# Thresholds and row-sum scaling on GpSimd from the second batch on, and all query, key and value loads on SyncE's queue

## The chip, the cores and the metric

The kernel runs on one core of one Trainium2 chip. The metric is the device time of one execution in microseconds (us). Three executions of the kernel before took 1327.75, 1332.97 and 1334.75 us; the median is 1332.97 us. The execution that was profiled took 1330.96 us, of which 1329.2 us lie between the first and the last instruction (the span).

Engine names are those of the profile: PE is TensorE's matmul, PEld its weight load, DVE is VectorE, ACT is ScalarE, POOL is GpSimd, SP is SyncE (SPq is SyncE's instruction queue).

## The reference

Attention over 8 batches, 8 heads, 576 positions and a head size of 64, in which only scores near the row's maximum take part, and after it a two-layer network with a rational function between its layers:

```python
scores = (q @ k.T) / 8
thresh = max(scores, -1) - tau
scores = where(scores >= thresh, scores, -1e9)
attn = exp(scores - max(scores, -1))
attn = attn / (sum(attn, -1) + 1e-9)
x = (attn @ v)                       # 8 heads side by side: 4608 rows of 512
h = x @ w_in                         # 512 -> 2048
g = (a0 + a1*h + a2*h**2 + a3*h**3) / (1 + |b0|*|h| + |b1|*h**2 + 1e-6)
out = g @ w_out                      # 2048 -> 512
```

All of it in float32 from outside; inside, products are put together from float16 parts or done in float32.

## The kernel before

**Tiles.** Two heads are a pair (bp, 32 of them: 4 in each of 8 batches). A unit of attention is 128 query positions of both heads of a pair (t = 0 to 3), or the last 64 positions of both (t = 4, 128 rows in one). 8 batches x 4 pairs x 5 give 160 units, 20 of them in the first batch. A visit takes some of a pair's units one after another; each pair is visited twice but for the last pair of each batch, which has all its units in one visit. Each visit loads the pair's queries and keys anew (`load_ops`, L586); values are loaded once for each pair (`load_v_ops`, L628). There are 2 buffers for queries, 2 for keys, 5 for values.

**A unit, in order** (`unit_ops`, L711). PE computes the scores of both heads into three banks of PSUM (L753, L757; L744 for t = 4). DVE takes both rows' negative maxima (L763 for 2 values a row, L765 for 1). The **threshold** `f_thr` (L767) turns the two maxima of each row into a bias: a multiply and an add on 128 x 2 values, on ACT (L770) or DVE (L772). ACT applies the steep Prelu that keeps what lies above the threshold (L778, one for each head; it frees the scores' banks), and the exponential with its row sums (L782). The **scaling of the sums** `f_rec` (L784) adds 1e-9 and multiplies by 2^-14, again 128 x 2 values, on ACT (L787) or DVE (L789); DVE then takes the reciprocal (L793). From the second batch on, the weights times the reciprocal are split into two float16 parts (`hi`: L300 on ACT or L302 on DVE; `lo`: L804 on DVE), SyncE transposes each by DMA into pT (L814), and PE multiplies with the values (L873). The first batch (`PLAIN`) does its transposes on PE.

From the 22nd unit on there is one set of banks for scores (`SINGLE`, L36), so the next unit's score product waits for both Prelus of the unit before it. There are 2 buffers for `hi`, 3 for the exponentials (which `lo` overwrites), 2 for pT.

**The network.** Beside the units, PE does the two layers for chunks of 256 rows (L987 first layer, L1058 and L1062 second), with the rational function on ACT and DVE between them (L996 to L1049). It begins in the first batch and its last chunks run after the last unit. Stores of the result are issued on GpSimd's queue (L1079, L1083).

**What sets the order.** All instructions are written out in the order that a planner (`Plan.order`, L148) finds before the kernel is built: a list schedule of all steps over the engines, with a duration for each step on each engine it may run on, latencies from one engine to the other (L109 to L111), and buffers. `FLEX` (L67) lists the steps that have more than one engine with their durations; the planner chooses. Loads and transposes on SyncE's queue are steps of a planned engine "DMA" (1.6 us for a load of queries or keys or values, 1.3 us for a transpose), DMAs issued by GpSimd are steps of a planned engine "GD" (the same 1.6 us for those loads), and arithmetic of GpSimd is a third, "POOL". On the chip "GD" and "POOL" are one in-order queue, and so is all of SyncE's.

**Where loads are issued.** `EARLY_BP = 8` (L48): pairs 0 to 7 (the first two batches) load on SyncE's queue, the later 24 pairs on GpSimd's. One group of loads for a visit is three DMAs for queries (L598 to L600), three for keys (L605 to L607) and, where the visit has the last 64 positions, two more for keys (L610); a pair's values are three DMAs (L636, L640 twice).

```python
        queue, eng = (nc.sync, "DMA") if bp < EARLY_BP else (nc.gpsimd, "GD")
```

In the first 140 us GpSimd's queue also issues the loads of the weights, and does a multiply of one element (L437) ahead of some of them, whose only purpose is to wait for an earlier load.

Of the kernel before, what the change touches and what calls it, by code (L numbers as in the profile page):

```python
# [15 lines left out]
ALU = mybir.AluOpType  # L16
# [28 lines left out]

NV = 5

EARLY_BP = 8  # L48

FROM_ACT = 2  # L50

# [6 lines left out]
UP = 2.0 ** -14  # L58
# [8 lines left out]
FLEX = {"f1": {"ACT": 0.567, "DVE": 0.335}, "f6": {"DVE": 0.6}, "s1": {"ACT": 0.648, "DVE": 0.396},  # L67
        "s2": {"DVE": 0.663}, "vmax": {"ACT": 0.697, "DVE": 0.729}, "thr": {"ACT": 0.242, "DVE": 0.122},
        "rec": {"ACT": 0.1, "DVE": 0.12}, "hi": {"ACT": 0.667, "DVE": 0.427}, "vh": {"ACT": 0.72, "DVE": 0.45},
        "vl": {"DVE": 0.795}, "xh": {"ACT": 0.264, "DVE": 0.335}, "xhr": {"ACT": 0.103, "DVE": 0.133},  # L70
        "ev": {"ACT": 0.465, "DVE": 0.6}, "ev1": {"ACT": 0.156, "DVE": 0.196}, "A": {"ACT": 0.583, "DVE": 0.341},
        "r": {"ACT": 0.666, "DVE": 0.4015}, "r2": {"DVE": 0.6075},
        "gh": {"ACT": 0.31, "DVE": 0.2}, "wh": {"ACT": 0.57, "DVE": 0.38}}
# [31 lines left out]
class Plan:  # L105
# [16 lines left out]
    def op(self, eng, dur, key, fn, after=(), take=(), drop=()):  # L122
        engs = {eng: dur} if isinstance(eng, str) else eng
        o = Op(engs, key, fn, [x for x in after if x is not None], list(take), list(drop))
        o.rank = self.rank
        self.ops.append(o)
        return o
# [123 lines left out]
def masked_attention_rational_ffn(  # L251
# [12 lines left out]
    nc = tc.nc  # L264
# [13 lines left out]
    plan = Plan()  # L278
    op = plan.op
# [8 lines left out]
    engines = {"ACT": nc.scalar, "DVE": nc.vector, "POOL": nc.gpsimd}  # L288
# [41 lines left out]
    qscale, taue = cv[:, 2:3], cv[:, 3:4]  # L330
# [151 lines left out]
    for i in range(NW):  # L482
        pieces = []
        for c in range(NC):
# [9 lines left out]
            o6, box = decode_ops(n, key, load, hold)  # L494
# [29 lines left out]
    for f in range(NF):  # L524
# [12 lines left out]
        o, box = decode_ops(NC * NW + f, key, load, hold)  # L537
# [48 lines left out]
    def load_ops(bp, ts):  # L586
# [6 lines left out]
        p0 = p - (4.6 if first else 4.0)  # L593
        queue, eng = (nc.sync, "DMA") if bp < EARLY_BP else (nc.gpsimd, "GD")

# [32 lines left out]
    def load_v_ops(bp):  # L628
        bb, pr = divmod(bp, NP)
        plan.rank = pos[(bb * NP, 0)]  # L630
        vhold = vh_[bp] = Hold("v", NT // 2 + 1)
        queue, eng = (nc.sync, "DMA") if bp < EARLY_BP else (nc.gpsimd, "GD")

# [77 lines left out]
    def unit_ops(bp, t):  # L711
        bb, pr = divmod(bp, NP)
# [3 lines left out]
        heads = (0, 1) if full else (0,)  # L716
        kh, qh = kq[bp]
        plain = is_plain(bp, t)
        nh = len(heads)
        name = f"{bp}_{t}"  # L720
        box = {"s": {}}
# [37 lines left out]
        def f_max(hh):  # L759
            if "st" not in box:  # L760
                box["st"] = place(st_hold)
            if hh is None:
                nc.vector.tensor_reduce(box["st"][:, 0:2], box["both"], AX.X, ALU.max, negate=True)  # L763
            else:
                nc.vector.tensor_reduce(box["st"][:, hh:hh + 1], box["s"][hh], AX.X, ALU.max, negate=True)  # L765

        def f_thr(h0, h1):  # L767
            d, m = box["st"][:, 2 + h0:2 + h1], box["st"][:, h0:h1]
            if plan.eng == "ACT":
                nc.scalar.activation(d, m, AF.Identity, scale=qscale, bias=taue)  # L770
            else:
                nc.vector.tensor_scalar(d, m, qscale, taue, ALU.mult, ALU.add)  # L772

        def f_pre(hh):

# [4 lines left out]
        def f_sum(hh):  # L780
            e = box["e"][:, hh * S:(hh + 1) * S]
            nc.scalar.activation(e, e, AF.Exp, bias=ntau, accum_out=box["st"][:, 4 + hh:5 + hh])  # L782

        def f_rec():  # L784
            r = box["st"][:, 6:6 + nh]
            if plan.eng == "ACT":
                nc.scalar.activation(r, box["st"][:, 4:4 + nh], AF.Copy, scale=UP, bias=1e-9 * UP)  # L787
            else:
                nc.vector.tensor_scalar(r, box["st"][:, 4:4 + nh], 1e-9, UP, ALU.add, ALU.mult)  # L789

        def f_rec2():
            r = box["st"][:, 6:6 + nh]
# [101 lines left out]
        ex, mk = {}, {}  # L894
        need = k_done[bp] + q_done[bp]
        qk = op("PE", 1.47 if full else 1.12, p, f_qk, need, [sh[0]], [kh, qh] * nh)
        if full:
            mx = op("DVE", 1.255, p + 0.1, lambda: f_max(None), [qk], [st_hold])
        else:
            mx = op("DVE", 0.668, p + 0.1, lambda: f_max(0), [qk], [st_hold])  # L900
        thr = dict.fromkeys(heads, op(FLEX["thr"], 0, p + 0.15, lambda: f_thr(0, nh), [mx]))
        for hh in heads:
            ex[hh] = op("ACT", 0.716, p + 0.2 + 0.02 * hh, lambda hh=hh: f_pre(hh),
                        [thr[hh]] + ([ex[0]] if hh else []), [e_hold] if hh == 0 else (), [sh[hh]])
        for hh in heads:
            mk[hh] = op("ACT", 0.76, p + 0.3 + 0.02 * hh, lambda hh=hh: f_sum(hh), [ex[hh]])
        rec = op(FLEX["rec"], 0, p + 0.4, f_rec, list(mk.values()))
        rec = op("DVE", 0.075, p + 0.4, f_rec2, [rec])
        if plain:
            pieces = (0, 1, 2) if full else (0, 2)  # L910
# [245 lines left out]
    for bp, ts in visits:  # L1156
        load_ops(bp, ts)
        if (bp, ts) == visits[0]:
            for o in first_loads:
                o.after += k_done[0] + q_done[0]  # L1160
        for t in ts:
            unit_ops(bp, t)
# [18 lines left out]
    p = 0.0  # L1181
    for ck, fs in order:
        kind, bb, c = ck
        last = [(bp, t) for bp in range(NBP) for t in range(NT + 1) if x_chunk(bp // NP, t)[0] == ck]
        ready = max(pos[x] for x in last) + LEAD
        for f in fs:
            p = max(p + (SPACE0 if bb == 0 else SPACING), ready)
# [4 lines left out]
    ck, f, _, p = todo.pop()  # L1192
# [52 lines left out]
```

## Time and profile before

| | us |
|---|---|
| median of three executions | 1332.97 |
| the profiled execution | 1330.96 |
| its span | 1329.2 |
| PE busy | 1289.2 |
| DVE busy | 1227.2 |
| ACT busy | 1178.4 |
| POOL busy (with its DMA issues) | 249.7 |

The profile gives for each group of instructions its line, engine, operation, operands, shape, count, busy time and mean duration, and the idle time of the engine before it with what ended that. A view of waits sums that idle time by who waited for whom. A timeline lists instructions by start time. Busy times of a view by windows are in us, with the count of instructions in brackets. PE's ends are modelled, so a PE that is busy is not always at its peak.

### The profile page before, as it was taken

The page shows a single profiled execution, that of the slowest core. Times are in us where ns is not written, and L with a number is a line of the kernel's source. Part 1 is how long each engine was busy: PE and PEld are TensorE (multiplying, and loading weights), DVE is VectorE, ACT ScalarE, POOL GpSimd, SP SyncE. Part 2 cuts the span into 40 slices and gives each one's busy share as a digit, 9 for nine tenths or more (in the row PEclk, how much of TensorE's full clock was granted, in tenths as well). Part 3 has the DMA queues.
Part 4 walks back from the last instruction along what each step waited for, and adds up shares of the span by engine and source line. Part 5 has one row for each costly group of instructions (what it writes and reads, how often), then busy time and mean ns, then how long its engine had stood idle before and what let it go on. Part 6 is the DMA issues. An engine that isn't in the chain of part 4 may idle for free. (4 is left out here: it accounts for less than half of the span.)

```text
span 1329.2 us, 24899 instructions
## 1 busy us (share of the span) xinstructions
PE 1289.2 (97%) x9144; PEld 872.1 (66%) x9144; DVE 1227.2 (92%) x2043; ACT 1178.4 (89%) x2166; POOL 249.7 (19%) x476
## 2 busy tenths in 40 slices
PE   8989999999999999999998999999999999999997
PEld 6657666666666666666666666667666766677684
DVE  6979899999999999999998899999999999977875
ACT  6979899999988999999998799999999999985583
POOL 3110000012213230332113231332122221100000
PEclk9989999999999999999999999999999999999999
DMA  8441545566555575666646465756756655550000
GB/s 252 146 140 53 172 82 91 119 142 127 130 100 116 124 126 105 132 148 104 116 101 126 92 123 105 145 115 127 115 123 120 125 116 120 93 91 0 17 17 16
DMA packets 340202, 146.63 MB, mean 110 GB/s; under 512 B 316208, under 2 KB 323184, under 8 KB 340080
## 3 DMA queue, kind: packets, MB, share of 16 engines
q1 hardware_dynamic: 315504, 84.92, 36.5%
q0 software_dynamic: 23296, 58.88, 16.2%
q8 instruction: 72, 1.18, 0.4%
q10 hardware_dynamic: 1280, 1.25, 0.4%
q14 instruction: 50, 0.41, 0.1%
HBM read 60.30 MB, written 9.44 MB: 52 GB/s over the span
## 5 line engine op out<-in xcount | busy, mean ns | idle before, releaser
L987 PEld LDWEIGHTS <-wi 128*128 128x128 f16 x3456 | 334.0, 98 | 73.0 <-issue 35.1
L987 PE MATMUL banks<-x,wi 128*128 128x256 f16 x3072 | 361.3, 273 | 3.3 <-ACT t L996 2.7
L1062 PE MATMUL banks<-wp,t 128*128 128x512 f32 x576 | 278.9, 600 | 3.6 <-DVE t L1041 3.5
L1058 PE MATMUL banks<-wp,g 128*128 128x512 f32 x864 | 275.7, 449 | 2.1 <-DVE g L1049 1.6
L778 ACT ACTIVATE e<-banks,st,cf 128x576 f32<-128x576 f32 x288 | 235.2, 830 | 15.7 <-DVE st L772 12.6
L782 ACT ACTIVATE e<-e,cf 128x576 f32<-128x576 f32 x288 | 222.0, 779 | 0.1
L804 DVE SCALAR_TENSOR_TENSOR e<-e,st,hi 128x576 f16<-128x576 f32 x252 | 204.3, 811 | 7.6 <-ACT hi L300 6.6
L1058 PEld LDWEIGHTS banks<-wp,g 128*128 128x128 f32 x864 | 158.2, 189 | 78.1 <-issue 38.6
L763 DVE TENSOR_REDUCE st<-banks 128x2 f32<-128x1152 f32 x128 | 172.1, 1345 | 10.1 <-PE banks L757 9.0
L300 ACT ACTIVATE hi<-e,st 128x576 f16<-128x576 f32 x199 | 151.6, 769 | 30.3 <-DVE st L793 20.7
L753 PE MATMUL banks<-KK,QQ 64*128 64x512 f32 x512 | 153.5, 645 | 1.9 <-ACT e L778 1.7
L1062 PEld LDWEIGHTS banks<-wp,t 128*128 128x128 f32 x576 | 101.2, 190 | 73.5 <-issue 59.4
L996 ACT ACTIVATE t<-banks,hsc 128x512 f32<-128x512 f32 (+1 forms) x192 | 106.3, 576 | 24.6 <-PE banks L987 24.3
L873 PEld LDWEIGHTS <-V 128*64 128x64 f16 x2520 | 103.0, 111 | 29.8 <-issue 27.1
L873 PE MATMUL banks<-pT,V 128*64 128x256 f16 (+1 forms) x2520 | 120.8, 249 | 0.9 <-DMA pT<-e 0.9
L757 PEld LDWEIGHTS banks<-KK,QQ 128*128 128x128 f32 x256 | 38.2, 188 | 97.8 <-issue 88.7
L598 POOL DMA_DIRECT2D QQ<-in_qT_dram x42 | 22.6, 539 | 424.5 <-PE banks L744 255.2
L1041 DVE SCALAR_TENSOR_TENSOR t<-t,cf,t 128x1024 f32<-128x1024 f32 (+1 forms) x73 | 92.3, 1265 | 0.8
L1032 DVE SCALAR_TENSOR_TENSOR t<-t,cf,t 128x1024 f32<-128x1024 f32 (+1 forms) x73 | 92.2, 1264 | 0.5
L1035 DVE SCALAR_TENSOR_TENSOR t<-t,t 128x1024 f32<-128x1024 f32 (+1 forms) x73 | 87.8, 1203 | 3.4 <-ACT t L1029 3.4
L307 DVE TENSOR_TENSOR t<-t,t 128x1024 f32<-128x1024 f32 (+1 forms) x73 | 87.8, 1203 | 1.6 <-ACT t L1015 1.2
L1023 DVE TENSOR_TENSOR t<-t,t 128x1024 f32<-128x1024 f32 (+1 forms) x73 | 87.8, 1203 | 1.0 <-ACT t L1008 0.8
(124 smaller groups left out, 1820.4 us busy)
## 6 DMA issues: line engine op xcount, KB each, us to landing
t<-in_w_in_dram POOLq DMA_DIRECT2D x16, 512.0 KB, 5.5
t<-in_w_out_dram POOLq DMA_DIRECT2D x16, 512.0 KB, 4.6
out_dram<-u POOLq DMA_DIRECT2D x30, 256.0 KB, 3.0
V<-in_v_dram POOLq DMA_DIRECT2D x24, 256.0 KB, 4.1
QQ<-in_qT_dram POOLq DMA_DIRECT2D x42, 144.0 KB, 2.8
KK<-in_kT_dram POOLq DMA_DIRECT2D x42, 144.0 KB, 3.0
QQ<-in_qT_dram POOLq DMA_DIRECT2D x42, 128.0 KB, 2.7
KK<-in_kT_dram POOLq DMA_DIRECT2D x42, 128.0 KB, 2.7
```

The costliest lines, as they stand in the source:

```text
L300: nc.scalar.activation(dst, src, AF.Identity, scale=factor)
L753: nc.tensor.matmul(d, QQ[r, t * P:(t + 1) * P], KK[r, REM:S], **one)
L763: nc.vector.tensor_reduce(box["st"][:, 0:2], box["both"], AX.X, ALU.max, negate=True)
L778: nc.scalar.activation(ev(hh), box["s"][hh], AF.Prelu, scale=qscale, bias=box["st"][:, 2 + hh:3 + hh], alpha=STEEP)
L782: nc.scalar.activation(e, e, AF.Exp, bias=ntau, accum_out=box["st"][:, 4 + hh:5 + hh])
L804: nc.vector.scalar_tensor_tensor(box["lo"][:, c], ev(hh), box["st"][:, 6 + hh:7 + hh], box["hi"][:, c], ALU.mult, ALU.subtract)
L873: nc.tensor.matmul(dst, V[:, c * P + hh * D:c * P + (hh + 1) * D], rhs, start=c == 0 and n == 0, stop=c == NT and n == 2)
L987: nc.tensor.matmul(d, wi_tile(c, f0 + j, hl), x[:, c, :], start=c == 0 and n == 0, stop=c == NC - 1 and n == 2)
L996: nc.scalar.activation(box["h3"][:, 2 * k:2 * k + 2, sl], psv[:, :, sl], AF.Identity, scale=hsc[:, b2, g:g + 1])
L1041: nc.vector.scalar_tensor_tensor(box["r"], box["r"], a0, box["q"], ALU.add, ALU.mult)
L1058: nc.tensor.matmul(acc[tt], fr(g[:, x]), fr(wo[f][y]), start=begins and j == n == 0, stop=ends and j == nb - 1 and n == 2)
L1062: nc.tensor.matmul(acc[tt], box["r"][:, o:o + P], wo[f], start=begins and j == 0, stop=ends and j == nb - 1)
```

## The change

GpSimd does the threshold and the scaling of the sums from the second batch on: the planner gets no other engine for them, and is given 0.5 us for each. The first batch keeps the choice between ACT and DVE. `EARLY_BP` becomes 32, which is all pairs: all loads of queries, keys and values go to SyncE's queue, among the transposes. (The keys of the first two pairs stay on ACT's queue, as before.) The planner is given no other new number, and plans all steps anew.

```diff
-EARLY_BP = 8
+EARLY_BP = 32
...
             if plan.eng == "ACT":
                 nc.scalar.activation(d, m, AF.Identity, scale=qscale, bias=taue)
             else:
-                nc.vector.tensor_scalar(d, m, qscale, taue, ALU.mult, ALU.add)
+                engines[plan.eng].tensor_scalar(d, m, qscale, taue, ALU.mult, ALU.add)
...
             if plan.eng == "ACT":
                 nc.scalar.activation(r, box["st"][:, 4:4 + nh], AF.Copy, scale=UP, bias=1e-9 * UP)
             else:
-                nc.vector.tensor_scalar(r, box["st"][:, 4:4 + nh], 1e-9, UP, ALU.add, ALU.mult)
+                engines[plan.eng].tensor_scalar(r, box["st"][:, 4:4 + nh], 1e-9, UP, ALU.add, ALU.mult)
...
-        thr = dict.fromkeys(heads, op(FLEX["thr"], 0, p + 0.15, lambda: f_thr(0, nh), [mx]))
+        thr = dict.fromkeys(heads, op(FLEX["thr"] if bb == 0 else {"POOL": 0.5}, 0, p + 0.15, lambda: f_thr(0, nh), [mx]))
...
-        rec = op(FLEX["rec"], 0, p + 0.4, f_rec, list(mk.values()))
+        rec = op(FLEX["rec"] if bb == 0 else {"POOL": 0.5}, 0, p + 0.4, f_rec, list(mk.values()))
         rec = op("DVE", 0.075, p + 0.4, f_rec2, [rec])
```

## The prediction

> **What bounds the kernel now.** I read the page first, then busy time by windows, then the waits of PE, then the lines that the change touches, and last the timeline around the transposes.
>
> ```profile
> span 1329.2 us, 24899 instructions
> PE 1289.2 (97%) x9144; PEld 872.1 (66%) x9144; DVE 1227.2 (92%) x2043; ACT 1178.4 (89%) x2166; POOL 249.7 (19%) x476
> ```
>
> PE is busy 97% of the span. The windows (columns: window, length, then busy us and count for PE, PEld, DVE, ACT, POOL, then granted clock, DMA share, GB/s) show where the rest lies.
>
> ```profile
> 0.00:165.00 165.00, 148.44 (x998) 105.86 (x1000) 140.23 (x325) 138.51 (x297) 25.08 (x64) 0.97 0.51 154
> 165.00:1185.00 1020.00, 1006.13 (x7326) 668.74 (x7321) 982.85 (x1596) 955.16 (x1744) 219.78 (x403) 1.00 0.60 116
> 1185.00:1329.00 144.00, 134.68 (x827) 97.45 (x824) 104.09 (x123) 84.74 (x129) 4.83 (x9) 0.99 0.07 20
> 165.00:285.00 120.00, 116.48 (x863) 79.37 (x858) 115.47 (x193) 112.62 (x210) 7.65 (x13) 1.00 0.53 103
> 285.00:1185.00 900.00, 889.64 (x6464) 589.37 (x6463) 867.38 (x1404) 842.54 (x1536) 212.13 (x391) 1.00 0.61 118
> ```
>
> The changed steps belong to batches 1 to 7, which run from about 165 to 1185 us. PE idles 1020 - 1006.13 = 13.9 us there. The 16.6 us of the head and the 9.3 us of the tail hold hardly a changed step. So the change can win at most about 14 us; what it can lose is open. DVE idles only 1020 - 982.85 = 37.2 us in this section and ACT 64.8 us, so both stand close behind PE. Within the section the first 120 us stand out: there PE idles 3.5 us, against 10.4 us in the 900 us behind.
>
> What PE waits for in the section (us in total, times, longest):
>
> ```profile
> PE banks L987 <- ACT t L996: 6.0, 5, 3.4
> PE banks L1062 <- DVE t L1041: 2.2, 3, 1.1
> PE banks L1058 <- DVE g L1049: 1.6, 2, 0.8
> PE banks L753 <- ACT e L778: 1.1, 2, 0.8
> PE banks L385 <- DVE u L381: 1.0, 2, 0.7
> PE banks L873 <- DMA pT<-e: 0.9, 1, 0.9
> PE banks L1058 <- DVE g L294: 0.5, 1, 0.5
> PE banks L857 <- ACT pT L292: 0.2, 1, 0.2
> ```
>
> 12.6 us name ACT or DVE, 0.9 us a transpose. The score product, which waits for the Prelus and so stands behind the threshold, holds PE up in only 2 places (1.1 us).
>
> **The change, part by part.** First, what leaves ACT and DVE (count, then min/median/max ns, in the section):
>
> ```profile
> L770 ACT ACTIVATE st<-st,cf x98: 368/376/397, 179.2 to 1181.3; 128x2 f32<-128x2 f32 x84, 128x1 f32<-128x1 f32 x14
> L772 DVE TENSOR_SCALAR st<-st,cf x40: 267/282/388, 209.8 to 1141.9; 128x2 f32<-128x2 f32 x26, 128x1 f32<-128x1 f32 x14
> L787 ACT ACTIVATE st<-st x85: 185/202/265, 169.1 to 1180.0; 128x2 f32<-128x2 f32 x66, 128x1 f32<-128x1 f32 x19
> L789 DVE TENSOR_SCALAR st<-st x55: 144/160/248, 208.3 to 1184.4; 128x2 f32<-128x2 f32 x46, 128x1 f32<-128x1 f32 x9
> ```
>
> ACT loses 98 x 0.376 + 85 x 0.202 = 54.0 us, DVE 40 x 0.282 + 55 x 0.160 = 20.1 us. None of it is PE's own time. It is worth only what PE idles because these two are late: the 12.6 us above less one wait of 3.4 us that has another cause (below), so between 0 and 9.2 us. ACT's idle time goes from 64.8 to 118.8 us and DVE's from 37.2 to 57.3 us, which makes being late rarer but not gone; half of it is my estimate: **-4.6 us**.
>
> Second, what GpSimd adds: 140 thresholds and 140 scalings (batches 1 to 7 have 7 x 20 units). The only rows of GpSimd arithmetic of like size are the one-element multiplies of the head; two more rows show a slow one and what DVE did at that time, two others bear on the chain:
>
> ```profile
> L437 POOL TENSOR_SCALAR cf<-t x13: 181/183/969, 15.7 to 136.1; 1x1 f32<-1x1 f32 x13
> ```
>
> ```profile
> 22.26 0.68 DVE L456 SCALAR_TENSOR_TENSOR u<-t,u 128x512 int32<-128x512 int32 x1
> 22.45 0.54 POOL L437 TENSOR_SCALAR cf<-t 1x1 f32<-1x1 f32 x1
> ```
>
> ```profile
> L804 DVE SCALAR_TENSOR_TENSOR e<-e,st,hi 128x576 f16<-128x576 f32 x251 | 203.5, 811 | 6.1 <-ACT hi L300 5.1 <-ACT g L292 0.3
> ```
>
> ```profile
> ACT hi L300 <- DVE st L793: 20.7, 36, 1.4
> ```
>
> So one costs between 0.18 and 0.97 us, plus a second crossing between engines: DVE to GpSimd to ACT for the threshold, ACT to GpSimd to DVE for the scaling. At the low end a threshold is sooner than the 0.376 us on ACT, at the high end 0.97 - 0.38 = 0.59 us later. The row at 22.45 us shows what makes the difference: it ends with DVE's two-operand instruction beside it (22.26 + 0.68 = 22.94; 22.45 + 0.54 = 22.99). DVE starts its next instruction as soon as the maximum is done, and that is often a two-operand one (L804 alone takes 203.5 us of the section), so long cases will be common. By the Trainium skill ("SBUF — State Buffer", section "SBUF: two separate sides") a GpSimd instruction that reads SBUF and a DVE instruction with two SBUF inputs exclude each other for the whole length of the one that started first; the trace agrees with that (0.54 us beside L456 against a median of 0.183).
>
> What lies on the path: the threshold delays ACT's Prelus, and these PE's next score product. PE idles there at 2 of 140 units now. If 5 more units came late by 0.59 us, PE would lose 3 us; at 20 it would be 12 us; fewer than now is possible too, as the planner allows more for the step than it did. I take the low count, since 2 is so few: **+3 us**, ends -1.1 (the wait at the score product gone) and 12. The scaling delays ACT's `hi`, for whose input ACT already idles 20.7 us in 36 places; that is not PE's time as long as ACT and DVE keep their slack (the third rival is the case where they don't). Behind a waiting threshold or scaling stand, on GpSimd's queue, only the next ones and the stores, for which nobody waits but the buffers of the result.
>
> Third, the loads move from GpSimd's queue to SyncE's: 42 visits (7 in each of batches 2 to 7) and 24 pairs' values.
>
> ```profile
> POOL QQ L598 <- PE banks L744: 255.2, 24, 33.9
> SPq L814 <- PE banks L873: 55.6, 21, 12.2
> ```
>
> ```profile
> L598 POOL DMA_DIRECT2D QQ<-in_qT_dram x42: 522/524/894, 284.2 to 1141.1; - x42
> ```
>
> On GpSimd these loads stood up to 33.9 us before PE freed their buffer. A threshold could not stand behind that, so the two parts of the change go together. On SyncE's queue the same wait stands ahead of transposes, and a transpose that waits for PE to free pT (up to 12.2 us) stands ahead of loads. The planner orders both by its own clock, so only what runs off plan costs. Batch 1 shows it, as its loads are on SyncE's queue already:
>
> ```profile
> 245.45 0.47 SPq L598 DMA_DIRECT2D QQ<-in_qT_dram  x1
> ...
> 249.15 1.23 SPq L610 DMA_DIRECT2D KK<-in_kT_dram  x2
> 250.49 2.49 SPq L814 DMA_TRANSPOSE pT<-hi  x1
> ...
> 258.88 1.39 PE L873 MATMUL banks<-pT,V 128*64 128x256 f16 x22 [0.91 <-DMA pT<-e]
> ```
>
> Eight issues hold the queue from 245.45 to 250.38 us, 4.9 us where the planner counts 2 x 1.6 = 3.2. The next transpose starts right behind them, is itself held up (2.49 us), and PE stands 0.91 us for pT. It is the only time in the section that PE waits for a transpose. Between 165 and 285 us there are 4 such groups on SyncE's queue, so 0.91 / 4 = 0.23 us for each; for 42 groups **+9.5 us**. The lower end is 0 (one case in four could be chance), the upper is the second rival's.
>
> What goes with GpSimd's loads is this kind of collision:
>
> ```profile
> 718.74 0.83 POOL L636 DMA_DIRECT2D V<-in_v_dram  x1
> ...
> 720.10 2.19 SPq L814 DMA_TRANSPOSE pT<-e  x1
> 722.39 2.92 SPq L814 DMA_TRANSPOSE pT<-hi  x1
> 725.80 0.77 ACT L300 ACTIVATE hi<-e,st 128x576 f16<-128x576 f32 x1 [3.71 <-DMA pT<-hi]
> 727.41 0.80 PE L987 MATMUL banks<-xr,wi 128*128 128x256 f16 x3 [3.37 <-ACT t L996]
> ```
>
> Values loaded by GpSimd and transposes by SyncE run at once; the transposes are slow, ACT stands 3.71 us for a buffer of `hi`, and PE 3.37 us for ACT. This is a quarter of all PE idle time in the section. Planned on one queue the two can't start at once, so I take it out: **-3.4 us** (ends -3.4 and 0). What stays of such collisions on one queue is in the 0.23 us, a rate from where all loads for queries and keys were there. By the Trainium skill ("DMA: Bandwidth & Descriptors", section "Issuing engines are not separate DMA queues") DMAs run on the same 16 engines and interleave whoever issues them, so that moving the issue takes no bytes out of the transposes' way; by that rule the last term would be 0 and the sum 3.4 us higher. The slow transposes at 720 and 250 us, one beside GpSimd's loads and one behind SyncE's, speak for it.
>
> The sum: -4.6 + 3.0 + 9.5 - 3.4 = +4.5 us. Against the profiled execution that is 1330.96 + 4.5 = 1335.5 us. The median of the runs is 2.0 us above that execution, so 1337.5 us, 0.3% above 1332.97. A measurement of this kernel can tell about 0.5% (6.7 us) from no change, since three runs lie within 7 us; so the forecast is no difference that can be told, on the slower side. Its own range is 1331 to 1340.
>
> **The rivals.** *Faster: PE's waits go.* The lighter ACT and DVE end all 9.2 us of waits that name them, the collisions go (3.4), and neither GpSimd nor SyncE is late: 1332.97 - 12.6 = 1320.4 us. For it: ACT loses 54 us, more than all its idle time names. Against it: PE idles 13.9 us altogether in the section, so nearly all of it would have to be had, and the planner's new order brings its own small waits. Chance 0.27.
>
> *Slower: SyncE's queue is the new wait.* Its place is a load group ahead of a transpose, its price PE's wait for pT or for the buffers of `hi`. If the whole section idles as its first 120 us do, PE loses 900 x 3.52 / 120 = 26.4 us where it lost 10.4, so +16: 1349 us. It decides from about 0.30 us for a load group: with the other three terms at -5.0, 42 x 0.28 = 11.7 us are needed to reach +6.7. For it: those 120 us are the only place with this arrangement. Against: they hold the change from batch 0 to 1 as well, and only 0.9 of their 3.5 us name a transpose. Chance 0.21.
>
> *Slower: DVE waits for GpSimd and becomes the bound.* Its place is the reciprocal (L793), which now stands on DVE's in-order queue behind a scaling on GpSimd. Without the moved work DVE has 982.85 - 20.1 = 962.7 us in the section. If it stands 0.54 us (the row at 22.45 us) before each of 140 reciprocals, that makes 1038 us, 18 us more than the section has: 1351 us. It decides from (1006.1 - 962.7) / 140 = 0.31 us for a unit, where DVE is even with PE. The rule on SBUF above makes it likelier. Against: a scaling that is held up by a DVE instruction ends with it, so DVE seldom waits for the whole of it. Chance 0.14.
>
> That the change does not do what it says is no case here: the planner has GpSimd as the only engine for these steps, and all 32 pairs are under the new bound.
>
> **How the numbers follow.** The forecast (1331 to 1340) has 0.38, which is the chance of within 0.5%. Faster by more has the first rival's 0.27, slower the other two's 0.35. The range goes from the first rival's time, 1320 (half of its chance lies above), to 1351, the third's; some 0.2 is left out.
>
> **What would show it.** Right or wrong by step: no L770, L787, L772 or L789 behind about 165 us, and ACT's busy time 54 us lower with DVE's 20 us lower. GpSimd's TENSOR_SCALAR at L770's and L787's places with medians between 0.2 and 0.8 us and a tail that ends with DVE's two-operand instructions. PE's waits that name a transpose in several places in place of one; none of 3 us behind values loaded by GpSimd. PE's idle time between 165 and 1185 us near 18 us. The prediction is wrong if that idle time falls below 8 us or goes above 22, if DVE's waits for GpSimd pass 40 us, or if the head or the tail changes by more than 3 us.

## The result and the profile after

The changed kernel takes 1422.70 us (median of 6 runs, 1412.60 to 1428.34) against 1333.40 us (6 runs): a ratio of 1.067, 95% interval 1.065 to 1.070. It is 89 us slower. The profiled execution took 1416.67 us.

The page of the changed kernel, as far as it answers to the lines shown of before:

```profile
span 1414.9 us, 24957 instructions
PE 1329.1 (94%) x9144; PEld 885.7 (63%) x9144; DVE 1230.6 (87%) x1953; ACT 1146.5 (81%) x1976; POOL 320.0 (23%) x384
...
L778 ACT ACTIVATE e<-banks,st,cf 128x576 f32<-128x576 f32 x288 | 235.1, 831 | 130.8 <-POOL st L772 118.4
...
L772 POOL TENSOR_SCALAR st<-st,cf 128x2 f32<-128x2 f32 (+1 forms) x140 | 207.0, 1479 | 304.8 <-DVE st L763 232.8
...
L753 PE MATMUL banks<-KK,QQ 64*128 64x512 f32 x512 | 175.7, 650 | 33.1 <-ACT e L778 33.0
...
L789 POOL TENSOR_SCALAR st<-st 128x2 f32<-128x2 f32 (+1 forms) x140 | 65.0, 464 | 501.8 <-ACT e L782 501.7
```

Two lines of before, to set beside L778 and L753:

```profile
L778 ACT ACTIVATE e<-banks,st,cf 128x576 f32<-128x576 f32 x288 | 235.2, 830 | 15.7 <-DVE st L772 12.6
L753 PE MATMUL banks<-KK,QQ 64*128 64x512 f32 x512 | 153.5, 645 | 1.9 <-ACT e L778 1.7
```

No engine but GpSimd has much more work than before: ACT is busy 32 us less, DVE 3 us more, PE has the same 9144 matmuls. PE's idle time in the whole span rose from 1329.2 - 1289.2 = 40.0 to 1414.9 - 1329.1 = 85.8 us. The other 40 us are in PE's busy time, which grew without more work: 22 us of it in L753 (153.5 to 175.7 us for the same 512 matmuls; the four of a unit took 1.2 us on average before, and in the row at 838.13 us below, where they stop between the two heads for a bank, they count as 2.33 us). The chain can be read from the lines: a threshold on GpSimd takes 1479 ns on average, ACT stands 118.4 us for it, PE stands 33.0 us for ACT. The scaling, also a multiply and an add on 128 x 2 values, takes 464 ns.

By windows (columns as before), the section of the changed steps is long and thin. Its last scaling starts at 1263.8 us, so the second window holds all but its end:

```profile
0.00:165.00 165.00, 148.40 (x1004) 105.73 (x1006) 140.77 (x325) 139.00 (x297) 25.85 (x66) 0.97 0.52 154
165.00:1250.00 1085.00, 1026.52 (x7218) 671.43 (x7214) 966.73 (x1480) 913.98 (x1541) 284.52 (x304) 0.99 0.54 108
1250.00:1415.00 165.00, 154.16 (x928) 108.54 (x926) 123.11 (x150) 93.50 (x140) 9.65 (x15) 0.97 0.11 23
```

The head is as it was (148.40 us of PE work against 148.44). Between 165 and 1250 us PE idles 58.5 us, and what it waits for in its first 1020 us is this:

```profile
PE banks L753 <- ACT e L778: 30.1, 29, 3.3
PE banks L987 <- ACT t L996: 9.9, 10, 1.7
PE banks L873 <- DMA pT<-e: 5.5, 6, 2.7
PE banks L1062 <- DVE t L1041: 5.1, 6, 2.7
PE banks L744 <- ACT e L778: 3.0, 3, 1.8
```

The score product waits for the Prelus in 29 places where it waited in 2 (30.1 us in place of 1.1). One unit of the timeline shows how:

```profile
831.20 1.35 DVE L763 TENSOR_REDUCE st<-banks 128x2 f32<-128x1152 f32 x1
...
832.46 0.81 DVE L804 SCALAR_TENSOR_TENSOR e<-e,st,hi 128x576 f16<-128x576 f32 x1
...
832.72 4.49 POOL L772 TENSOR_SCALAR st<-st,cf 128x2 f32<-128x2 f32 x1 [4.59 <-DVE st L763]
...
833.19 0.41 DVE L1049 TENSOR_TENSOR g<-t,g 128x256 fp32r<-128x256 f32 x1
...
833.52 1.22 DVE L307 TENSOR_TENSOR t<-t,t 128x1024 f32<-128x1024 f32 x1
...
834.66 1.22 DVE L1023 TENSOR_TENSOR t<-t,t 128x1024 f32<-128x1024 f32 x1
835.79 1.28 DVE L1032 SCALAR_TENSOR_TENSOR t<-t,cf,t 128x1024 f32<-128x1024 f32 x1
837.24 1.55 ACT L778 ACTIVATE e<-banks,st,cf 128x576 f32<-128x576 f32 x2 [4.21 <-POOL st L772]
...
838.13 2.33 PE L753 MATMUL banks<-KK,QQ 64*128 64x512 f32 x4 [2.66 <-ACT e L778]
```

The maximum ends at 832.55 us. DVE has begun its next instruction by then; the threshold starts 0.17 us later and does not end before five two-operand instructions of DVE have passed, four of which began after it. They take what they always take (0.81, 0.41, 1.22, 1.28 us). It ends at 837.21 us. ACT has stood 4.21 us, PE stands 2.66, and DVE itself finds no new scores for its next maximum until 841.29 us.

### The profile page after: what moved, and what is told of

It is laid out like the page before. It is cut to its first block, busy times and chain, and to the rows that moved or that the text cites. A ratio compares the mean times of both kernels' runs of the same rounds, so it can differ in the third digit from the quotient of the medians.

```text
span 1414.9 us, 24957 instructions
## 1 busy us (share of the span) xinstructions
PE 1329.1 (94%) x9144; PEld 885.7 (63%) x9144; DVE 1230.6 (87%) x1953; ACT 1146.5 (81%) x1976; POOL 320.0 (23%) x384
## 5 line engine op out<-in xcount | busy, mean ns | idle before, releaser
L987 PEld LDWEIGHTS <-wi 128*128 128x128 f16 x3456 | 336.9, 100 | 81.0 <-issue 39.9
L987 PE MATMUL banks<-x,wi 128*128 128x256 f16 x3072 | 372.3, 277 | 8.8 <-ACT t L996 7.8
L778 ACT ACTIVATE e<-banks,st,cf 128x576 f32<-128x576 f32 x288 | 235.1, 831 | 130.8 <-POOL st L772 118.4
L1062 PE MATMUL banks<-wp,t 128*128 128x512 f32 x576 | 280.3, 603 | 8.3 <-DVE t L1041 8.2
L1058 PE MATMUL banks<-wp,g 128*128 128x512 f32 x864 | 282.3, 456 | 0.1
L772 POOL TENSOR_SCALAR st<-st,cf 128x2 f32<-128x2 f32 (+1 forms) x140 | 207.0, 1479 | 304.8 <-DVE st L763 232.8
L804 DVE SCALAR_TENSOR_TENSOR e<-e,st,hi 128x576 f16<-128x576 f32 x252 | 204.7, 812 | 7.5 <-ACT hi L300 6.4
L753 PE MATMUL banks<-KK,QQ 64*128 64x512 f32 x512 | 175.7, 650 | 33.1 <-ACT e L778 33.0
L789 POOL TENSOR_SCALAR st<-st 128x2 f32<-128x2 f32 (+1 forms) x140 | 65.0, 464 | 501.8 <-ACT e L782 501.7
L300 ACT ACTIVATE hi<-e,st 128x576 f16<-128x576 f32 x184 | 140.7, 770 | 28.5 <-issue 12.2
L1062 PEld LDWEIGHTS banks<-wp,t 128*128 128x128 f32 x576 | 102.1, 192 | 79.7 <-issue 60.5
L753 PEld LDWEIGHTS banks<-KK,QQ 64*128 64x128 f32 x512 | 50.9, 186 | 91.6 <-ACT e L778 71.0
L1026 ACT ACTIVATE t<-t,cf 128x1024 f32<-128x1024 f32 (+1 forms) x73 | 82.6, 1131 | 17.1 <-DVE t L1023 17.1
L1041 DVE SCALAR_TENSOR_TENSOR t<-t,cf,t 128x1024 f32<-128x1024 f32 (+1 forms) x73 | 92.2, 1263 | 0.9
```

Of the source, the lines that this page charges most:

```text
L300: nc.scalar.activation(dst, src, AF.Identity, scale=factor)
L753: nc.tensor.matmul(d, QQ[r, t * P:(t + 1) * P], KK[r, REM:S], **one)
L772: engines[plan.eng].tensor_scalar(d, m, qscale, taue, ALU.mult, ALU.add)
L778: nc.scalar.activation(ev(hh), box["s"][hh], AF.Prelu, scale=qscale, bias=box["st"][:, 2 + hh:3 + hh], alpha=STEEP)
L804: nc.vector.scalar_tensor_tensor(box["lo"][:, c], ev(hh), box["st"][:, 6 + hh:7 + hh], box["hi"][:, c], ALU.mult, ALU.subtract)
L987: nc.tensor.matmul(d, wi_tile(c, f0 + j, hl), x[:, c, :], start=c == 0 and n == 0, stop=c == NC - 1 and n == 2)
```

## The experiments

Theory A: GpSimd's threshold is late, since its reads of SBUF are held up by DVE; ACT waits for it, and through the one set of score banks PE. Rivals: B, the loads among the transposes on SyncE's queue (the prediction's own suspect); C, the order that the planner made anew. Ratios are to runs of the kernel before on the same chip, with 95% intervals.

**DVE does the steps, in the changed kernel's order.**

```diff
-                engines[plan.eng].tensor_scalar(d, m, qscale, taue, ALU.mult, ALU.add)
+                nc.vector.tensor_scalar(d, m, qscale, taue, ALU.mult, ALU.add)
...
-                engines[plan.eng].tensor_scalar(r, box["st"][:, 4:4 + nh], 1e-9, UP, ALU.add, ALU.mult)
+                nc.vector.tensor_scalar(r, box["st"][:, 4:4 + nh], 1e-9, UP, ALU.add, ALU.mult)
```

> The order on every engine's queue stays that of the changed kernel, and all loads stay on SyncE's queue; only the 140 thresholds and 140 scalings of batches 1 to 7 are issued to DVE in place of GpSimd. Theory A (GpSimd's threshold is slow, 1.48 us a piece in the changed kernel, and holds up ACT and through it PE): DVE does a threshold in 0.28 us, so most of the 89 us go; 1330 to 1350 us. Theory B (loads among the transposes on SyncE's queue): nothing that it names has changed; 1400 to 1420 us. Theory C (the order that was planned anew is bad by itself): as B, 1400 to 1420 us.

Measured: 1364.02 us, ratio 1.026 (1.023 to 1.029). More than half of the loss goes with GpSimd; B and C could carry the rest at most. A's range is missed by 14 us. Part of the rest may be of the experiment's own making: DVE does some 62 us of instructions (140 x (0.283 + 0.162)) that the planner had not given it. Its busy time, in which instructions that overlap count once, rises by 29 us to 1260.0 us. What that costs was not measured.

**The threshold's numbers stand in the instruction.** This kernel does not read tau; its output is that of the reference for this case's tau alone.

```diff
-                engines[plan.eng].tensor_scalar(d, m, qscale, taue, ALU.mult, ALU.add)
+                (engines[plan.eng].tensor_scalar(d, m, 0.125, 0.02, ALU.mult, ALU.add) if plan.eng == "POOL" else
+                 nc.vector.tensor_scalar(d, m, qscale, taue, ALU.mult, ALU.add))
```

> The changed kernel, but GpSimd's threshold has its factor 0.125 and its addend 0.02 as numbers in the instruction, where the changed kernel reads them from SBUF for each row (so tau is fixed at the value that this case has). Theory A1 (each separate read of SBUF by GpSimd can be held off by a DVE instruction with two SBUF operands; the threshold has three reads, the scaling one): the threshold's mean falls from 1.48 us to about 0.5 us, like the scaling's 0.46, and the time to 1340 to 1370 us. Theory A2 (the threshold is slow because of where it stands, right behind the maximum when DVE begins a run of such instructions, however many reads it has): mean above 1.1 us, time 1400 us or more. Theories B and C (queue, order): time 1400 to 1420 us whatever the threshold takes.

Measured: 1355.49 us, ratio 1.020 (1.017 to 1.024). Two reads of one value for each row cost some 63 us: the kernel is 26 us above the one before, where the changed kernel is 89 above it. The lines of this run: the threshold and the scaling in the view by lines, the threshold's durations (min/median/max ns), and ACT's wait for it:

```profile
L772 POOL TENSOR_SCALAR st<-st 128x2 f32<-128x2 f32 (+1 forms) x140 | 102.8, 734 | 308.6 <-DVE st L763 235.8 <-DVE st L794 43.9 <-DVE st L765 22.0
L790 POOL TENSOR_SCALAR st<-st 128x2 f32<-128x2 f32 (+1 forms) x140 | 85.6, 612 | 519.7 <-ACT e L783 519.4
```

```profile
L772 POOL TENSOR_SCALAR st<-st x140: 182/620/3227, 160.0 to 1201.2; 128x2 f32<-128x2 f32 x112, 128x1 f32<-128x1 f32 x28
```

```profile
ACT e L779 <- POOL st L772: 46.6, 45, 4.2
```

The threshold's mean falls from 1479 to 734 ns and ACT's wait for it from 118.4 to 46.6 us. So A1 holds in direction and in most of its size, but not wholly: at 734 ns it is still longer than A1's 0.5. How much of that is the place right behind the maximum (A2) is not shown; the scaling, which has another place and now as many reads, takes 612 ns in this run.

**The threshold alone, and the scaling alone**, each with all loads on SyncE's queue and a new plan:

```diff
-        rec = op(FLEX["rec"] if bb == 0 else {"POOL": 0.5}, 0, p + 0.4, f_rec, list(mk.values()))
+        rec = op(FLEX["rec"], 0, p + 0.4, f_rec, list(mk.values()))
```

> Thresholds on GpSimd from the second batch on, all loads on SyncE's queue, but the scalings back on ACT and DVE by the planner's choice. Theory A: the threshold carries nearly all of the loss; 1400 to 1420 us. If the scaling had a share of its own (DVE waits 28.8 us for it in the changed kernel): 1380 to 1395 us.

Measured: 1408.85 us, ratio 1.060 (1.056 to 1.064). The scaling alone is the same edit at `thr` in place of `rec`:

> Scalings on GpSimd from the second batch on, all loads on SyncE's queue, but the thresholds back on ACT and DVE by the planner's choice. Theory A: 1330 to 1345 us, since a scaling takes 0.46 us and only the reciprocal waits for it. Theory B (SyncE's queue): 1390 us or more, as the loads are where the change put them.

Measured: 1342.35 us, ratio 1.010 (1.006 to 1.014). The threshold carries six of the 6.7%. B is out as the cause of the loss: here the loads are where the change put them, and 13 us are lost, not 89.

**The loads alone, in the order of before.** The planner plans as before, with these loads on its engine "GD", and only their issue moves; all compute engines have the same instructions in the same order as before. The line stands twice in the kernel, and both are changed.

```diff
-        queue, eng = (nc.sync, "DMA") if bp < EARLY_BP else (nc.gpsimd, "GD")
+        queue, eng = (nc.sync, "DMA") if bp < EARLY_BP else (nc.sync, "GD")
```

> The kernel before, its order on every compute engine unchanged and thresholds and scalings where they were; only the loads of batches 2 to 7 are issued on SyncE's queue, at the places in the order where GpSimd issued them. Theory A (GpSimd's threshold carries the loss): 1328 to 1340 us. Theory B (the prediction's term of 0.23 us for each of 42 load groups, less the collision that goes): about 1336 us; its rival with the whole section like batch 1: 1347 us. In the run with the scalings alone, PE's waits that name a transpose were 2.7 us; near that here too if they come from the queue.

Measured: 1333.72 us, ratio 1.001 (0.999 to 1.003): no difference. PE's waits in the section, and ACT's for a buffer of `hi`:

```profile
PE banks L873 <- DMA pT<-e: 5.5, 6, 2.0
PE banks L987 <- ACT t L996: 4.3, 5, 1.7
...
PE banks L873 <- DMA pT<-hi: 0.8, 1, 0.8
```

```profile
ACT hi L300 <- DMA pT<-hi: 0.4, 1, 0.4
```

Both of the prediction's load terms are there, and nearly cancel. PE waits for transposes in 7 places (6.3 us, where it was 0.9 in one), and the stop of 3.4 us behind GpSimd's values is gone (the longest wait of L987 is 1.7 us).

**The scaling alone, in the order of before**, with the loads as in the last run:

```diff
-            if plan.eng == "ACT":
+            if bb:
+                nc.gpsimd.tensor_scalar(r, box["st"][:, 4:4 + nh], 1e-9, UP, ALU.add, ALU.mult)
+            elif plan.eng == "ACT":
```

> As the run before this one, and the scalings of batches 1 to 7 are issued to GpSimd at the places where ACT or DVE did them; the planner knows nothing of it. If the 1.0% of the scaling-alone run came from the new order: 1325 to 1335 us here, no slower than with the loads alone. If GpSimd's scaling costs time by itself (0.5 us, then DVE's reciprocal behind it): 5 to 15 us above the loads alone, with DVE's wait for GpSimd near 20 us.

Measured: 1334.11 us, ratio 1.002 (1.001 to 1.004), as the loads alone. GpSimd's scaling (mean 613 ns, DVE's wait for it 11.0 us) costs nothing that shows beside the loads alone (1.001). That the planned order cost the scaling-alone run its other 0.8% follows only by subtraction: the two differ in the order, and in the engines that the planner chose for other steps.

**One of the two numbers read.**

```diff
-                engines[plan.eng].tensor_scalar(d, m, qscale, taue, ALU.mult, ALU.add)
+                (engines[plan.eng].tensor_scalar(d, m, 0.125, taue, ALU.mult, ALU.add) if plan.eng == "POOL" else
+                 nc.vector.tensor_scalar(d, m, qscale, taue, ALU.mult, ALU.add))
```

> The changed kernel with the threshold's factor 0.125 as a number in the instruction and only the addend read from SBUF for each row. Theory A1 (each read by itself can be held off): half-way between the changed kernel and the run with both numbers in the instruction: shortest threshold 0.26 us (0.34 and 0.18 there), median 0.8 us (1.05 and 0.62), time 1375 to 1395 us. Theory A2 (any read from SBUF beside the data takes the long way, once): like the changed kernel, 1405 us or more.

Measured: 1386.91 us, ratio 1.042 (1.039 to 1.045), half-way. The threshold by lines, and its durations:

```profile
L772 POOL TENSOR_SCALAR st<-st,cf 128x2 f32<-128x2 f32 (+1 forms) x140 | 159.6, 1140 | 307.8 <-DVE st L763 234.8 <-DVE st L794 43.6 <-DVE st L765 22.3
```

```profile
L772 POOL TENSOR_SCALAR st<-st,cf x138: 256/934/4781, 186.4 to 1232.1; 128x2 f32<-128x2 f32 x110, 128x1 f32<-128x1 f32 x28
```

With none, one and two reads beside the data the shortest threshold takes 182, 256 and 336 ns, the mean 734, 1140 and 1479, and the run 1355, 1387 and 1423 us. Each read costs 74 to 80 ns when nothing holds it, 340 to 410 ns as things are, and 28 and 35 us of the whole (26, 54 and 89 us above the kernel before, each measured beside it).

**The planner is told 1.5 us.**

```diff
-        thr = dict.fromkeys(heads, op(FLEX["thr"] if bb == 0 else {"POOL": 0.5}, 0, p + 0.15, lambda: f_thr(0, nh), [mx]))
+        thr = dict.fromkeys(heads, op(FLEX["thr"] if bb == 0 else {"POOL": 1.5}, 0, p + 0.15, lambda: f_thr(0, nh), [mx]))
```

> The changed kernel, but the planner is told 1.5 us for a threshold on GpSimd, its measured mean, in place of 0.5. If the loss comes from an order planned for thresholds that are there sooner: most of it goes, 1340 to 1365 us. If it comes from the long way from the maximum to the Prelus as such (one set of score banks, so the next score product waits): 1390 to 1420 us.

Measured: 1402.35 us, ratio 1.053 (1.051 to 1.055). The price of the mean wins back 20 us of 89. No other price was tried. A single figure stands here for something that takes 0.33 to 5.1 us, which may be why most of the loss stays.

**The threshold alone in the order of before**, with the loads on SyncE's queue: first reading both numbers, as below; then with 0.125 and 0.02 in place of `qscale` and `taue`; then that with the scaling on GpSimd too, by the edit of the scaling alone above:

```diff
-            if plan.eng == "ACT":
+            if bb:
+                nc.gpsimd.tensor_scalar(d, m, qscale, taue, ALU.mult, ALU.add)
+            elif plan.eng == "ACT":
```

> The order of the kernel before on all compute engines, loads on SyncE's queue (0.1% by itself), and the thresholds of batches 1 to 7 issued to GpSimd with both numbers read from SBUF; scalings on ACT and DVE. Theory A: the threshold's long way costs by itself, whatever order was planned; 1380 to 1410 us, mean threshold 1.3 to 1.6 us. Theory C (it took the new order too): under 1360 us.

Measured: 1405.39 us, ratio 1.055 (1.053 to 1.058). The old order loses nearly as much as the new one, so C is not needed for most of the loss. The threshold by lines:

```profile
L770 POOL TENSOR_SCALAR st<-st,cf 128x2 f32<-128x2 f32 (+1 forms) x140 | 209.3, 1495 | 832.5 <-DVE st L763 574.8 <-DVE st L795 130.0 <-DVE st L765 70.6
```

> As the run before this one, with the threshold's 0.125 and 0.02 as numbers in the instruction. Theory A1: median threshold about 0.6 us, time 1335 to 1350 us, under the 1355 us that the new order with both steps gave.

Measured: 1344.42 us, ratio 1.009 (1.007 to 1.011). The median threshold takes 692 ns; by lines:

```profile
L770 POOL TENSOR_SCALAR st<-st 128x2 f32<-128x2 f32 (+1 forms) x140 | 100.0, 714 | 875.1 <-DVE st L763 608.9 <-DVE st L795 139.3 <-DVE st L765 73.9
```

> Both steps of batches 1 to 7 on GpSimd in the old order, the threshold's numbers in the instruction, loads on SyncE's queue: the whole change, less the new order and less the two reads. ACT and DVE are relieved of 54 and 20 us. If relief is worth what the prediction gave it (4.6 us): some 5 us under the run with the threshold alone. If it is worth nothing, as PE is the bound: the same or up to 5 us above.

Measured: 1346.67 us, ratio 1.011 (1.009 to 1.013). Taking another 17 us off ACT and 9 us off DVE wins nothing; the interval overlaps with that of the threshold alone. None of these versions beats the kernel before. With the same steps and numbers, but in the newly planned order and with the engines that the planner then chose, it was 1.020 (1.017 to 1.024): C does cost something, some 11 us.

**The scaling reads its numbers too**, set against the run with the scaling alone in the order of before:

```diff
+    nc.vector.memset(two_c[:, 0:1], 1e-9)
+    nc.vector.memset(two_c[:, 1:2], UP)
...
-                nc.gpsimd.tensor_scalar(r, box["st"][:, 4:4 + nh], 1e-9, UP, ALU.add, ALU.mult)
+                nc.gpsimd.tensor_scalar(r, box["st"][:, 4:4 + nh], two_c[:, 0:1], two_c[:, 1:2], ALU.add, ALU.mult)
```

> As the scaling alone in the old order (1334 us, GpSimd's scaling 0.18 us at the shortest, median 0.48), but its two numbers 1e-9 and 2^-14 are read from SBUF for each row. Theory A1 for the duration: shortest 0.34 us, median about 1.0, as the threshold has them. For the time: only DVE's reciprocal waits for the scaling, so DVE's wait for GpSimd goes from 11 to some 30 us, and the time to 1340 to 1355 us; as much as the threshold costs (1390 us or more) only if GpSimd slows DVE or ACT in another way than by being late.

Measured: 1342.12 us, ratio 1.008 (1.006 to 1.011), against 1.002 without the reads. The scaling by lines, its durations, and DVE's wait for it:

```profile
L790 POOL TENSOR_SCALAR st<-st,two_c 128x2 f32<-128x2 f32 (+1 forms) x140 | 121.1, 865 | 872.7 <-ACT e L785 799.0 <-DVE t L1028 15.6 <-DVE x L894 13.4
```

```profile
L790 POOL TENSOR_SCALAR st<-st,two_c x140: 331/724/2485, 170.3 to 1197.1; 128x2 f32<-128x2 f32 x112, 128x1 f32<-128x1 f32 x28
```

```profile
DVE st L798 <- POOL st L790: 27.3, 74, 2.7
```

The shortest is as expected. The median (0.72 us) is not 1.0. A scaling starts when ACT is done, at any point of DVE's work, while a threshold starts just as DVE begins its next instruction; that this is the reason was not tested. And the two reads cost 8 us here where they cost 61 at the threshold (1405 against 1344). Part of that is that they lengthen the scaling by less: its mean goes from 613 to 865 ns, 35 us in all, where the threshold's goes from 714 to 1495, 109 us in all. A microsecond of it costs 8 / 35 = 0.23 us at the scaling and 61 / 109 = 0.56 at the threshold, so it also counts who waits.

**DVE stands still while the threshold runs.** That DVE holds the reads was until here only seen side by side. There is one execution of each kernel here, so no interval. The threshold is as in the run of 1405 us, but it is issued right behind the maximum, and then DVE must copy a value out of its result before it goes on.

```diff
+            if bb:
+                nc.gpsimd.tensor_scalar(box["st"][:, 2:2 + nh], box["st"][:, 0:nh], qscale, taue, ALU.mult, ALU.add)
+                nc.vector.tensor_copy(dve_waits[:, 0:1], box["st"][:, 2:3])
...
+            if bb:
+                return
```

> As the threshold alone in the old order (1405 us, both numbers read from SBUF, mean 1.50 us), but the threshold is issued right behind the maximum, and DVE's next instruction copies a value out of it, so DVE waits until it is done. If DVE's instructions with two SBUF operands are what holds its reads up: 0.33 to 0.40 us for nearly all 140, median and mean. If it is slow for another reason (where its data lie, the crossing from DVE, transfers): the mean stays above 1 us. For the time: DVE stands about 0.25 + 0.34 + 0.2 us for each of 140 units, 110 us of which some 57 fit its idle time; 1370 to 1410 us.

Measured: 1403.13 us against 1331.73. The threshold's durations, and who waited for it:

```profile
L768 POOL TENSOR_SCALAR st<-st,cf x140: 334/345/348, 161.2 to 1254.9; 128x2 f32<-128x2 f32 x112, 128x1 f32<-128x1 f32 x28
...
  DVE dve_waits L769: 77.3, 140
```

All 140 thresholds take 334 to 348 ns. So it is DVE's work that holds them up. The time is no better: it is now DVE that stands, 77.3 us, where it had 37.2 us of idle time in the section before and 11.3 us less to do. PE's longest wait is now for DVE, at the second layer's product (L1062 of before; 21.2 us in 30 places).

## Why the prediction was wrong

The sum was +4.5 us, the measured +89, far outside the range. PE's idle time from 165 to 1185 us became 56.2 us, where the prediction had named 22 as the sign that it is wrong. By the prediction's steps:

- **What bounds the kernel: right.** PE is the bound, the changed section alone moves, the gain is bounded and the loss open.
- **Relief of ACT and DVE (-4.6 us): no run showed any.** In the old order the kernel was no faster with both steps off ACT and DVE than with one (1.011 and 1.009), nor with the scaling off them than with the loads alone (1.002 and 1.001); each of these runs has GpSimd's lateness in it too. In the changed kernel ACT's busy time fell by 32 us and not 54, and DVE's did not fall: the planner moved other steps.
- **What GpSimd adds (+3 us, ends -1.1 and 12): this step failed.** It took a one-element multiply with its numbers in the instruction as "of like size", and from it 0.18 to 0.97 us. The threshold reads two more values for each row. Its mean alone, 1.48 us, lies outside that range and its longest at 5.1. The prediction had the row that shows one read held up by one DVE instruction, and the rule for it, and it did not count the threshold's reads. The next link failed with it: 5 units of 140 were taken to be late, as PE waited at 2 of them before; that count belonged to a threshold that took 0.28 or 0.38 us. ACT stood for it 88 times, 118.4 us in all. By the runs in the old order the threshold with reads costs 72 us (1405 against 1334 with the loads alone), with its numbers in the instruction 11. Added up from runs that were each set beside the kernel before: the two reads some 63 us, the new order 11, the threshold without these reads 11, the scaling 2 and the loads 1, which is 88 of the 89.
- **Loads on SyncE's queue (+9.5 - 3.4 us): the mechanism right, the net too large.** Alone they cost 0.1% (-0.1 to 0.3), where the two terms gave 6 us. The stops for pT came (7, where one was), but they add 5.4 us and not 9.5; the stop behind GpSimd's values went.
- **The rivals.** The faster one did not come: no version beat the kernel before. The one on SyncE's queue fell with the loads alone. The one on GpSimd had the mechanism, and put it in the wrong place: DVE does wait at the reciprocal (28.8 us in 26 places, under the 40 that the prediction named as a sign), but that is cheap; the costly wait is ACT's at the Prelu, since the next score product stands behind it.
- **The two rules taken from the Trainium skill.** The one on the shared ports ("SBUF — State Buffer", section "SBUF: two separate sides") was the one to follow further: with one wait for DVE behind each read in mind, the steps should have been compared by their reads. By the other ("DMA: Bandwidth & Descriptors", section "Issuing engines are not separate DMA queues") DMAs interleave on the same 16 engines whoever issues them, and the last term would have been 0. The run with the loads alone is 1 us above the kernel before (1.001, 0.999 to 1.003), too little to tell the two apart; the one stop of 3.4 us did go.

What stays open: why the newly planned order costs more than the old one (0.8% with the scaling alone, 0.9% with both steps and the numbers in the instruction); and how the 40 us that PE's busy time grew by divide between stops inside a product and a lower clock (the granted clock is 0.982 of full speed in the changed kernel, 0.993 before).

## What to carry to other kernels

Before a small step goes to GpSimd beside a busy DVE, count its reads of SBUF, the per-row numbers among them, and look at what DVE does in just that moment: here each read cost 0.08 us alone and 0.34 to 0.41 us on average beside DVE's work. Price it by who waits for it: a microsecond of lateness cost 0.56 us of the whole in front of the step that frees the only score banks, and 0.23 us in front of a reciprocal. And when an engine is the bound with 14 us to win, relief for its neighbours is no reason to lengthen a chain that ends at it.

## What the runs showed of the hardware that was not expected

- A GpSimd instruction that waits for DVE can be passed by DVE more than once. At 832.72 us a two-operand instruction of DVE (L804) was running when the threshold began. Four more began after the threshold, each before the one ahead of it had ended, and ran their usual time; the threshold ended behind the last. DVE as a whole was not slowed (L804: 812 ns on average, 811 before).
- The number of reads bears on how often. Here is one place of the same order, in the run with the numbers in the instruction and in the changed kernel:

```profile
321.19 0.51 DVE L302 TENSOR_SCALAR hi<-e,st 128x576 f16<-128x576 f32 x1
...
321.43 0.32 POOL L772 TENSOR_SCALAR st<-st 128x2 f32<-128x2 f32 x1 [1.93 <-DVE st L763]
321.61 0.81 DVE L805 SCALAR_TENSOR_TENSOR e<-e,st,hi 128x576 f16<-128x576 f32 x1
```

```profile
332.54 0.51 DVE L302 TENSOR_SCALAR hi<-e,st 128x576 f16<-128x576 f32 x1
...
332.80 1.04 POOL L772 TENSOR_SCALAR st<-st,cf 128x2 f32<-128x2 f32 x1 [1.94 <-DVE st L763]
332.97 0.82 DVE L804 SCALAR_TENSOR_TENSOR e<-e,st,hi 128x576 f16<-128x576 f32 x1
```

Without the two reads the threshold ends 0.05 us behind L302 (321.75 against 321.70), with them 0.05 us behind the instruction after it (333.84 against 333.79). Of the thresholds that began beside L302, 23 of 24 end 0.05 us behind it without the reads, and none of 30 with them. L302 reads one tensor and one value for each row, so it isn't only instructions with two tensors that hold GpSimd up.
- A threshold that comes in while DVE is idle is not held:

```profile
299.76 0.34 POOL L770 TENSOR_SCALAR st<-st,cf 128x2 f32<-128x2 f32 x1 [0.59 <-DVE st L763]
299.86 0.85 DVE L806 SCALAR_TENSOR_TENSOR e<-e,st,hi 128x576 f16<-128x576 f32 x1 [0.20 <-ACT hi L300]
```

This is from the threshold alone in the old order, with both reads. In the changed kernel it happened at 915.65 and 1086.66 us: 0.35 us each, though a two-operand instruction began 0.24 and 0.21 us after the threshold. In the five runs in which GpSimd reads both numbers in the loop and DVE goes on working (the changed kernel, the threshold alone in both orders, the price of 1.5 us, the scaling with reads) ten steps that began on an idle DVE, 0.09 to 0.32 us ahead of its next two-operand instruction, took 0.34 to 0.35 us; six that were ahead by less than 0.08 us took 0.93 to 1.52 us. Starts on GpSimd are rough in this profile, so these two figures are no exact limit.
- By the Trainium skill ("SBUF — State Buffer", section "SBUF: two separate sides") whichever of the two starts first holds the port pair for its whole instruction. The traces agree that GpSimd waits for a DVE instruction that is running, and that one which came in 0.09 us or more ahead of DVE is not held. At 832.72 us DVE was first, but the four instructions that began after the threshold passed it as well. Whether a waiting GpSimd instruction takes the ports anew for each read, no run settles.
- GpSimd's multiply and add on 128 x 2 values is short where nothing is in its way: 181 to 183 ns at the shortest, 256 with one value for each row read beside the data, 331 to 348 with two.
